# A segment-recurrent attention and ReGLU kernel laid out anew: leftover rows packed, transposes by DMA, memory sums in column quarters, an order searched offline

## The chip, the cores and the metric

The kernel runs on one core of a Trainium2 chip. The time is device microseconds of that core, taken over several executions. The profile is one execution recorded by the hardware profiler. PE is TensorE's matmul row, PEld its weight loads, DVE is VectorE, ACT ScalarE, POOL GpSimd, SP SyncE, whose queue issues the DMAs. A run on one core has no second die to compare with. All repeated runs here are recorded as of the fast state (granted clock 0.952 to 0.954 in the runs of the kernel before, 0.992 to 0.995 in those of the changed one); runs with a single execution are marked "one look", and their state is unknown.

Ratios are computed as the mean time of one kernel's runs over that of the other's of the same rounds, so they are not quite the ratio of the medians that are quoted.

## The reference, cut to what matters

```python
def _A_ref(x, mem0, Wq, Wk, Wv, Wo, seg_len):      # D = 448, H = 16 heads of 256, M = 8, seg_len = 32
    mem = mem0
    for s in range(n_seg):                          # 64 segments, one after the other
        h = concat([mem, x[:, s*32:(s+1)*32, :]])   # 40 rows
        q, k, v = h @ Wq, h @ Wk, h @ Wv
        p = softmax(where(mask, q @ k.T / 16, -1e9))
        o = (p @ v) @ Wo
        mem = o[:, :8, :]                           # the next segment needs it
        outs.append(o[:, 8:, :])
def _B_ref(x, W_gate, W_up, W_down):                # F = 1792
    gate = x @ W_gate
    return ((gate * (gate > 0)) * (x @ W_up)) @ W_down
x = x + _A_ref(layernorm(x), ...); x = x + _B_ref(layernorm(x), ...)    # layer 0
x = x + _A_ref(layernorm(x), ...); x = x + _B_ref(layernorm(x), ...)    # layer 1, the same weights
```

The eight memory rows make a recurrence over 64 segments. Everything else of a segment can wait. Both kernels form M = Wq Wk^T and N = Wv Wo per head during a setup phase. A step t then handles segment t of layer 0 together with segment t-4 of layer 1, so there are 68 steps. Two steps make a pair: 64 rows of each layer go through the sum over N and the gated unit together.

Names used below. `h` is a segment with its memory rows; `hT` is `h` with the features on the partitions, `hK` the same rows in natural layout, and T = M h. `Ps` and `Pm` are the softmax weights of the segment's rows and of the memory rows, `PTs` and `PTm` their transposes. U is these weights times `h`, before the sum over N (`Nw` in the trace); it lies in a large buffer called `big`, and the memory's own part in `UTm`. `XA` is the input of a layer's attention that is added back (the residual), `XB` is `XA` plus the attention's output, and `xn` and `xBT` are its LayerNorm, plain and transposed. The addition into XB ends a pair's sum over N and serves as the marker of a pair. A pitch is the time from one matmul's start to the next one's in an unbroken run. A change of tiling is a change of how the array is divided between matmuls. "Half clock" is time for which the trace's record of clock grants shows half the clock. A bias is a number added to the priority of one kind of group in the program's scheduler.

## The kernel before

The width 448 is three blocks of 128 rows and a leftover of 64. The kernel before pads the leftover with zeros to a fourth block (`kt = 3`):

```python
def t_unit(self, t, k):          # k = 0..6; T = M h for 8 of 56 blocks
    return [MM(v[:, j, l0 * KEYS:l0 * KEYS + n], S.M[:, kt, 8 * k + j, :],
               S.hT[:, pp, s, kt, l0:l1, :]..., start=(kt == 0), stop=(kt == 3))
            for j in range(8) for kt in range(4)]                      # 7 x 32 = 224 matmuls of 80 columns a step
```

The memory sum runs in four column tiles of the array; its four quarters are split into a high and a low half in bf16, and small matmuls with a selection matrix add and transpose them:

```python
def un_mem(self, t):
    for k in range(14):
        for j in range(4):
            o = 14 * j + k
            out.append(MM(b[32 * j:32 * j + 32, 0:D], lhs, S.N[:, o, :], start=(k == 0), stop=(k == 13)))
    ...
    S.act(... S.hi = copy of b ...)
    S.dve(... S.lo = b - S.hi ...)
def m_t(self, t): ...            # 8 matmuls selm x hi, lo: memory transposed, into the next hT
def m_nat(self, t): ...          # 2 matmuls of 448 columns with seln: memory in natural layout, into hK
```

The sum over N of a pair is 56 full matmuls, and all of them wait for all of U:

```python
def un(self, p):
    uk = [("U", s, l, c) for s in range(2) for l in range(2) for c in range(4)]
    for k in range(0, NO, 2):
        S.mm(lambda k=k: [MM(S.bO[:, 0:D], S.U[:, o, :], S.N[:, o, :], ...) for o in (k, k + 1)],
             2 * S.pitch(D), uk, S.ps(4))
```

Transposes of the LayerNorm outputs (`xn`), of the softmax weights (`Ps`) and, in the setup, of Wq, Wk and Wv are TensorE transposes with a copy out of PSUM each. PSUM is divided by hand: two pairs of banks for T, U and the gated unit (`R`), one bank for scores and transposes (`bG`), one for the long sums (`bO`), two for the memory (`bC`). A list scheduler in the program orders the groups once, when the kernel is built.

## Time and profile before

| | before |
|---|---|
| time, median | 1988.25 us (1987.97 to 1988.95, 3 runs) |
| PE / DVE / ACT busy | 92% / 51% / 39% of the span |
| first addition into XB (end of the setup and of pair 0) | 165.8 us |
| one pair of steps, mean of 24 steady pairs | 55.5 us |
| from the last XB to the end | 17.7 us |

The page's busy row and its strips, 40 equal slices of the span, the busy share in tenths (PEclk is the clock that the throttle granted):

```profile
PE 1825.2 (92%) x30992; PEld 1305.1 (66%) x30992; DVE 1013.9 (51%) x2529; ACT 771.0 (39%) x1960; POOL 94.3 (5%) x160
...
PE   7769999999999999999999999999999999999998
...
PEclk9869999999999999999999999999999999999999
```

TensorE is the bound, and only the setup is visibly thin. What a step costs TensorE is read from starts in the timeline: a matmul of 80 columns every 36.3 ns, of 448 every 190 ns. This is the timeline of TensorE at the turn from one pair to the next (start, duration, in brackets the idle time before it and who ended it):

```profile
1020.98 0.60 PE L127 MATMUL R<-PTs,hK 40*128 40x512 bf16 x4 [0.21 <-ACT PTs L709]
1022.96 0.39 PE L127 MATMUL R<-PTs,hK 40*128 40x512 bf16 x2 [1.38 <-DVE big L710]
1023.56 0.30 PE L127 MATMUL R<-PTs,hK 40*64 40x256 bf16 x4 [0.20 <-DVE big L710]
1024.71 1.65 PE L127 MATMUL bO<-Nw,big 128*128 128x448 bf16 x4 [0.85 <-DVE big L710]
```

Four waits within 4 us, 2.6 us in all; the last three are for copies of U (`big`). This returns in every pair; in the table of waits over the whole run it is the first two of these lines (total, times, longest; the third is a wait at another place, which section 1 needs):

```profile
PE R L127 <- DVE big L710: 47.4, 61, 1.4
PE bO L127 <- DVE big L710: 25.2, 31, 0.8
...
PE R L127 <- DVE xBT L710: 22.2, 32, 1.0
```

And this is the view of windows for the steady stretch from 500 to 1600 us (busy time of each engine, granted clock, DMA share, GB/s):

```profile
500.00:1600.00 1100.00, 1033.42 (x17910) 745.81 (x17908) 572.46 (x1404) 427.88 (x1094) 44.45 (x80) 0.96 0.02 4
```

TensorE is idle for 66.6 of 1100 us, 3.4 us a pair. The clock is 0.96 of full speed: the trace's record of clock grants has half-clock windows of 3.4 or 6.8 us about once a pair, 189 us of them in the whole run, 140 of these after the first 200 us (the setup has one of 27.3 us).

The windows lie on one grid of 3.41 us. From 300 us to 60 us before the end, 30 half-clock windows begin. In the 3.41 us of the grid just before, TensorE had stood idle for 1.65 to 2.44 us in 29 of these cases (0.94 in one); in no grid window that half clock did not follow had it been idle for more than 0.84 us. In this trace it is the sum of the short waits that sets the two kinds apart: no single wait between 300 and 1500 us was longer than 1.4 us.

### The profile page before, as it was taken

Reading aid. Unit: us, or ns where it says so; the run is one execution under the profiler, and the core shown is the slowest. Engines: PE = TensorE matmul, PEld = TensorE weight load, DVE = VectorE, ACT = ScalarE, POOL = GpSimd, SP = SyncE. Lnnn points to the kernel's source line nnn. Section 1 sums busy time; section 2 is a strip of 40 time slices with the busy share of each in tenths; the row PEclk is TensorE's granted clock in tenths of the full one; section 3 lists DMA queues with packets and bytes.
Section 4 is the critical chain, followed back from the end, with each engine's and each line's share of the span. In section 5 each row is a group of like instructions: output and inputs, shape, how many; then the busy total and the mean of one; then the engine's idle time right before and its main releaser. Section 6 shows DMA issues by size and latency. Waiting matters only on the chain.

```text
span 1986.3 us, 68251 instructions
## 1 busy us (share of the span) xinstructions
PE 1825.2 (92%) x30992; PEld 1305.1 (66%) x30992; DVE 1013.9 (51%) x2529; ACT 771.0 (39%) x1960; POOL 94.3 (5%) x160
## 2 busy tenths in 40 slices
PE   7769999999999999999999999999999999999998
PEld 5446776666666777666666677666666667766665
DVE  8623545554555544555554554455454555455432
ACT  6523333334343433333444443333344343333333
POOL 1020000000000000000000000000000000000000
PEclk9869999999999999999999999999999999999999
DMA  7400000000000000000000000000000000000000
GB/s 212 160 30 3 4 4 5 5 4 4 5 4 4 4 4 5 4 4 5 3 4 5 5 5 3 5 4 4 3 5 4 4 5 3 4 4 3 3 3 4
DMA packets 22303, 27.55 MB, mean 14 GB/s; under 512 B 5744, under 2 KB 15744, under 8 KB 22016
## 3 DMA queue, kind: packets, MB, share of 16 engines
q1 hardware_dynamic: 22016, 23.20, 4.0%
q8 instruction: 245, 4.01, 0.8%
q14 instruction: 42, 0.34, 0.1%
HBM read 21.35 MB, written 1.84 MB: 12 GB/s over the span
## 4 chain that ended last, share of the span: by engine, by line
PE 68%; DVE 17%; ACT 2%; issue 1%; DVEq 0%
PE R L127 35%; PE bO L127 22%; PE bC L127 8%; DVE big L710 7%; PE bG L127 2%; DVE stat L736 1%; DVE ys L1007 1%; DVE xn L743 1%; DVE XA L1003 1%; DVE hK L710 1%; DVE UTm L710 1%; DVE XB L978 1%; DVE Ps L870 1%; DVE hB L996 1%; DVE stat L868 1%
## 5 line engine op out<-in xcount | busy, mean ns | idle before, releaser
L127 PE MATMUL R<-hT,Mw 128*128 128x80 bf16 (+1 forms) x15232 | 548.7, 200 | 23.9 <-POOL hT L710 22.9
L127 PEld LDWEIGHTS R<-hT,Mw 128*128 128x128 bf16 x15232 | 539.7, 100 | 39.0 <-issue 24.0
L127 PE MATMUL bO<-Nw,big 128*128 128x448 bf16 x1904 | 463.5, 388 | 25.2 <-DVE big L710 25.2
L127 PEld LDWEIGHTS bO<-Nw,big 128*128 128x128 bf16 x1904 | 180.5, 105 | 201.4 <-issue 66.4
L127 PE MATMUL R<-xBT,big 128*128 128x128 bf16 x3808 | 251.7, 220 | 22.9 <-DVE xBT L710 22.2
L996 DVE TENSOR_TENSOR hB<-gT,R 128x256 bf16<-128x256 bf16 x238 | 100.0, 420 | 325.4 <-ACT gT L995 322.4
L127 PEld LDWEIGHTS R<-xBT,big 128*128 128x128 bf16 x3808 | 224.6, 98 | 46.2 <-DVE xBT L710 27.7
L127 PE MATMUL bC<-Nw,UTm 128*32 128x448 bf16 x3752 | 194.8, 360 | 3.0 <-ACT UTm L709 1.9
L709 ACT ACTIVATE TTs<-R 128x512 bf16<-128x512 f32 (+3 forms) x273 | 155.1, 568 | 107.8 <-PE R L127 107.8
L710 DVE CAST TTs<-R 128x512 bf16<-128x512 f32 (+3 forms) x271 | 176.4, 651 | 8.7 <-PE R L127 8.5
L995 ACT ACTIVATE gT<-R 128x256 bf16<-128x256 f32 x238 | 91.2, 383 | 183.4 <-PE R L127 179.5
L709 ACT ACTIVATE big<-R 128x512 bf16<-128x512 f32 (+1 forms) x263 | 134.6, 543 | 63.3 <-PE R L127 61.9
L710 POOL COPY hK<-xn 32x448 bf16<-32x448 bf16 x136 | 75.5, 555 | 1710.6 <-DVE xn L743 1659.1
L710 DVE CAST big<-R 128x512 bf16<-128x512 f32 (+1 forms) x249 | 148.7, 619 | 14.6 <-PE R L127 12.5
L710 DVE CAST TTm<-R 128x128 bf16<-128x128 f32 (+3 forms) x278 | 78.0, 281 | 151.2 <-PE R L127 138.8
L127 PEld LDWEIGHTS bC<-Nw,UTm 128*32 128x32 bf16 x3752 | 99.8, 98 | 83.6 <-ACT UTm L709 13.8
L127 PE MATMUL R<-PTs,hK 40*128 40x512 bf16 (+1 forms) x640 | 95.4, 352 | 57.8 <-DVE big L710 47.4
L709 ACT ACTIVATE hK<-bC 8x448 bf16<-8x448 f32 x96 | 51.4, 535 | 202.1 <-PE bC L127 200.5
L127 PE MATMUL bO<-big,hB 128*128 128x448 bf16 x476 | 129.2, 354 | 0.0
L127 PEld LDWEIGHTS R<-PTs,hK 40*128 40x128 bf16 (+1 forms) x640 | 26.4, 98 | 136.4 <-ACT big L709 57.7
L920 DVE TENSOR_TENSOR lo<-bC,hi 128x448 bf16<-128x448 f32 x67 | 41.5, 620 | 131.2 <-ACT hi L919 131.2
L709 ACT ACTIVATE TTm<-R 128x128 bf16<-128x128 f32 (+3 forms) x266 | 70.5, 265 | 70.6 <-PE R L127 70.6
(125 smaller groups left out, 1540.9 us busy)
## 6 DMA issues: line engine op xcount, KB each, us to landing
big<-in_A_Wo_dram SPq DMA_DIRECT2D x4, 896.0 KB, 5.7
big<-in_A_Wq_dram SPq DMA_DIRECT2D x4, 768.0 KB, 6.0
big<-in_A_Wk_dram SPq DMA_DIRECT2D x4, 768.0 KB, 7.8
big<-in_A_Wv_dram SPq DMA_DIRECT2D x4, 768.0 KB, 5.1
XA<-in_A_x_dram SPq DMA_DIRECT2D x32, 56.0 KB, 2.2
out_dram<-ys SPq DMA_DIRECT2D x32, 56.0 KB, 1.9
big<-in_B_W_down_dram SPq DMA_DIRECT2D x1, 1568.0 KB, 14.7
big<-in_B_W_gate_dram SPq DMA_DIRECT2D x1, 1344.0 KB, 7.3
```

The source lines that it names most:

```text
L127: ins = E.matmul(out, lhsT=lhsT, rhs=rhs, **kw)
L709: return E.activation(out(), src(), ACT.Copy)
L710: return E.tensor_copy(out(), src())
L736: S.dve(lambda E: E.bn_stats(st[:, so:so + 6], x), D, rd, [(key, 0)])
L743: S.dve(lambda E, a=a, b=b, src=src: E.tensor_scalar(S.xn[:, i, a:b], src, st[:, so + 6:so + 7], st[:, so + 8:so + 9], op0=ALU.subtract, o ...
L868: S.dve(lambda E: E.tensor_reduce(st[:, 48:48 + n], Sm, AX.X, ALU.add), w, [("Sm",)], [("ss", 1)])
L870: S.dve(lambda E: E.tensor_tensor(dst, Sm, bc(56), ALU.mult), w, [("Sm",), ("ss", 2)], [("Ps",)])
L920: S.dve(lambda E: E.tensor_tensor(S.lo[:, :], b[:, 0:D], S.hi[:, :], ALU.subtract), D, S.ps(6) + [("hi",)], [("lo",)])
L978: S.dve(lambda E: E.tensor_tensor(S.XB[:, p % 2, :], S.bO[:, 0:D], S.XA[:, p % 4, :], ALU.add), D, S.ps(4) + [("XA", p % 4, 0), ("XA", p % ...
L995: S.act(lambda E, k=k, R=R: E.activation(S.gT[:, k % 2, 0:256], R.b(0)[:, 0:256], ACT.Relu), 256, R.res(0), [("gT", k % 2)])
L996: S.dve(lambda E, k=k, R=R: E.tensor_tensor(S.hB[:, 2 * k:2 * k + 2, :].rearrange("p a b -> p (a b)"), S.gT[:, k % 2, 0:256], R.b(1)[:, 0: ...
L1003: S.dve(lambda E: E.tensor_tensor(S.XA[64:128, q % 4, :], S.bO[0:64, 0:D], S.XB[0:64, p % 2, :], ALU.add), D, S.ps(4, half=(0,)) + [("XB", ...
```

## The change

The same redesign is carried through in one step: leftover rows are packed in pairs, transposes move to DMA, the memory sums use column quarters, in 14 odd pairs the layer-1 sums ride along in spare columns, all eight PSUM banks form one pool, and the order is steered by biases per kind of group that were searched offline. The core of the diff, with cuts:

```diff
 # T units: 28 blocks x 2 heads; the leftover 64 rows of two heads side by side in the two halves of the array
-                    for j in range(8) for kt in range(4)]
+            def hm(Ts=Ts, a=a, z=z, o=o):
+                return [MM(o(Ts[st], j - a), S.M3[64 * st:64 * st + 64, j, :], hv(slice(64 * st, 64 * st + 64), 3 + st), start=(j == a))
+                        for j in range(a, z) for st in range(2)]
+                    return [MM(o(T, j - a), S.M[:, c, st, j, :], hv(full, c), stop=(c == 2)) for j in range(a, z) for c in range(3)]
...
 # memory sums
-            for k in range(14):
-                for j in range(4):
-                    o = 14 * j + k
-                    out.append(MM(b[32 * j:32 * j + 32, 0:D], lhs, S.N[:, o, :], start=(k == 0), stop=(k == 13)))
-        S.act(lambda E: E.activation(S.hi[:, :], b[:, 0:D], ACT.Copy), D, S.ps(6), [("hi",)])
-        S.dve(lambda E: E.tensor_tensor(S.lo[:, :], b[:, 0:D], S.hi[:, :], ALU.subtract), D, S.ps(6) + [("hi",)], [("lo",)])
+            return [MM(T.b()[32 * j:32 * j + 32, 0:224], S.UTm[:, o, :], S.N[:, o, 224 * (j % 2):224 * (j % 2) + 224], start=(k == 0), stop=(k == 27))
+                    for k in range(28) for j in range(4) for o in (28 * (j // 2) + k,)]
+        S.act("xE", lambda E: E.activation(S.XH[64:128, :], T.b()[64:128, 0:224], ACT.Copy), 224, T.res(BOTQ), [("XH",)])
+        for j in range(2):
+            S.dve("xE", ... S.X[r, c] = T.b()[r, 0:224] + S.XH[r2, :] ...)
...
 # transposes by DMA: hT to hK, Ps to PTs, xn to stg and xBT; in the setup Wq, Wk, Wv
+        S.dma("pts", "pts", lambda E: E.dma_start_transpose(S.PTs[:, :, :], S.Ps[:, :, :].rearrange("p a b -> p (a b)")), [("Ps",)], [("PTs",)],
+              1310.0, 2550.0)
...
 # sums over N: wait per chunk of U; in odd pairs only layer 0, two terms side by side, layer 1 rides in UTm[:, :, 16:32]
-        uk = [("U", s, l, c) for s in range(2) for l in range(2) for c in range(4)]
+                     2 * S.pitch(D), [("U", l, s, c_of(k)) for l in range(2) for s in range(2)] + nk, T.res())
+                S.mm("unc", lambda k=k: [MM(T.b()[64 * w:64 * w + 64, 0:D], S.U[:, o + w, cols], S.N[:, o + w, :], ...)
+                                         for o in (k, k + 2) for w in range(2)], ..., mode=COLS2)
...
 # the order, and waits that another wait implies are left out
+        for o in self.ops:
+            o.prio += BIAS.get(o.kind, 0.0)
+BIAS = {"dn": -2542.0, "dnE": -32472.0, ..., "lnaT": 13146.0, ..., "ys": 19174.0}
+            out.append((self.sems[src].sem, val))
+            for s2, v2 in self.clock[(src, val)].items():
+                if kn.get(s2, 0) < v2:
+                    kn[s2] = v2
```

The gated unit packs its leftover rows in the same way (98 instead of 112 matmul pitches).

## The prediction

> **What bounds the kernel now.** TensorE. In the page's busy row PE has 92% of the span, DVE 51%, ACT 39%. The XB additions (timeline) put the first at 165.8 us; then a pair of steps takes 55.3 us almost without variation, and 17.7 us follow the last. From matmul starts in the timeline (80 columns 36.3 ns, 128: 56, 448: 190, 40: 25), one step's own matmuls need 14.0 us: T units 224 x 36.3 = 8.1, memory sums 2.8, segment scores 0.9, U products 0.9, hi/lo copies and transposes the rest. A pair adds 10.6 (sums over Nw), 6.3 (gate/up), 2.7 (down), 0.5 (transposes): 48 us. About 18 changes of tiling at some 0.1 us (gap 1128.57 to 1128.68) make 50. The other 5.5 us are idle waits (XB, bank evictions before bO) and the halved clock (mean 0.94 to 0.96 in the windows).
>
> **What the change does, per steady pair.**
> - T units: the 64 leftover rows of D are row-packed, 224 full matmuls become 168 and 28 packed pairs: 7.1 instead of 8.1 us, -2.1 a pair. The trace shows such packing working: two row tiles (PTs,hK) start 3 ns apart. [...]
> - Gate/up the same way: 112 become 98 pitches, -0.8.
> - All transposes but Pm's, and the hi/lo gather, leave TensorE for DMA transposes and an fp32 addition: about -1.9.
> - Odd pairs: layer 1's rows ride in 16 unused columns of the memory sums, and layer 0's are column-packed: 28 pitches instead of 56, -2.6 on average.
> - Memory sums: 28 rounds of four 224-column tiles instead of 14 of 448: 2.7, unchanged. 112 small weight loads fit if they issue 3 ns apart as now.
> - More changes of tiling: 26 a pair in the built order, +0.7.
> Work falls from 50 to 43.5 us a pair, all on the PE path.
>
> **Other engines.** Evictions and softmax sum to about 25 us a step over DVE and ACT, some 12 of 23.5 each: not a bound. The recurrence, from hT to the next hT, is about 17 us with today's durations: shorter than a step. DMA transposes have no duration in this trace; [...] loads of x land in 2.2 us here. At 2 to 3 us they hide behind the T units.
>
> **Setup.** Now PE spends 384 transposes there with their evictions and ends in a 22.9 us wait (111 us)[...]. DMA transposes of Wq, Wk, Wv remove this; with Wo they move about 15 MB. First XB at 97 us, an estimate, instead of 166.
>
> **Sum.** 97 + 37 (second pair, one layer) + 30 x 46.6 + 72 (last two) + 17: about 1620 us, with 3 us a pair left for waits and clock instead of 5.5, since eight single banks and a searched order should leave fewer bank waits. If the 5.5 stay, 1695; with almost none, 1540.
>
> **What would show it.** Matmul group of hT,Mw down to 168 a step at the same 36 ns pitch; M3 pairs starting 3 ns apart; pairs alternating about 44 and 49 us; first XB near 97 us; transposes landing under 3 us; PE busy over 90% in the steady part and the chain of waits mostly PE.
>
> **What would make it wrong.** DMA transposes of 5 us or more, which lengthen the recurrence (hK before u, xBT before gate); column tiles of 224 limited by weight loads[...]; more half-clock windows from short PE gaps; a setup limited by slow DMA transposes of weights. None costs the 350 us saved.
>
> Chances: faster 0.97, same 0.02, slower 0.01.

## The result, and the profile after

The changed kernel takes 1567.84 us (1567.33 to 1569.21, 4 runs) against 1988.51 us in the same rounds: ratio 0.789, 95% interval 0.788 to 0.790. It is correct. The page of after, the lines that answer to those of before:

```profile
PE 1486.0 (95%) x33352; PEld 1150.6 (73%) x33352; DVE 710.6 (45%) x1892; ACT 808.3 (52%) x2388; POOL 91.0 (6%) x139
...
PE   3989999999999999999999999999999999999997
...
PEclk9899999999999999999999999999999999999999
```

The view of windows, 300 to 1400 us:

```profile
300.00:1400.00 1100.00, 1069.33 (x24233) 838.52 (x24233) 505.63 (x1328) 577.69 (x1687) 68.69 (x99) 1.00 0.18 27
```

TensorE is now idle for 30.7 of 1100 us, which is 1.25 us of a pair's 44.7 us, and the clock is full. Half-clock windows add up to 25.6 us in the run, where they were 189; none lies between 300 and 1500 us, where TensorE is idle for at most 1.7 us of any 3.41 us of the grid. No sharp limit can be read from the two traces: 1.65 to 2.44 us of idle time came before 29 of 30 half-clock windows there, and up to 1.7 us is followed by none here. The packed leftover rows in the timeline:

```profile
848.92 0.82 PE L134 MATMUL P<-hT,M 64*128 64x80 bf16 x36 [0.79 <-POOL hT L568]
849.67 4.04 PE L134 MATMUL P<-hT,Mw 128*128 128x80 bf16 x108
```

The 36 packed matmuls start in couples 3 to 4 ns apart, one couple every 36 ns, so 18 couples take 0.65 us; then 0.1 us passes to the next tiling (its first start is at 849.67).

The setup shows one fault. This is the timeline of the DMA queue (start, issue time):

```profile
1.39 3.53 SPq L624 DMA_TRANSPOSE big<-in_A_Wq_dram  x1
15.41 1.20 SPq L728 DMA_TRANSPOSE stg<-xnA  x1
16.65 3.55 SPq L624 DMA_TRANSPOSE big<-in_A_Wk_dram  x1
20.24 3.96 SPq L624 DMA_TRANSPOSE big<-in_A_Wq_dram  x1
```

Here the queue does not pass a waiting entry. Its third entry is the transpose of the first LayerNorm's output, which is not ready until 15.4 us, and the transposes of the weights stand behind it from 4.9 to 15.4 us. The first product starts at 22.3 us.

Where the 421 us went, by the XB additions in the timeline:

| stretch | before, us | after, us | estimate in the prediction, us |
|---|---|---|---|
| start to the first XB | 165.8 | 123.1 | 97 |
| first to second XB | 53.3 | 31.5 | 37 |
| second to last XB | 1749.4 | 1397.8 | 30 x 46.6 and 72 for the last two pairs, 1470 |
| last XB to the end | 17.7 | 14.9 | 17 |

### The profile page after: what moved, and what is told of

Same layout as the page of the kernel before. It is cut to its first block, busy times and chain, and to the rows that moved or that the text cites. A ratio compares the mean times of both kernels' runs of the same rounds, so it can differ in the third digit from the quotient of the medians.

```text
span 1567.3 us, 72227 instructions
## 1 busy us (share of the span) xinstructions
PE 1486.0 (95%) x33352; PEld 1150.6 (73%) x33352; DVE 710.6 (45%) x1892; ACT 808.3 (52%) x2388; POOL 91.0 (6%) x139
## 4 chain that ended last, share of the span: by engine, by line
PE 78%; DMA 10%; DVE 6%; ACT 3%; issue 1%; SPq 1%; POOL 1%; POOLq 0%; DVEq 0%
PE P L134 78%; DMA stg<-xnA 4%; DMA PTs<-Ps 4%; ACT big L567 2%; DVE big L568 1%; SPq L624 1%; DVE stat L714 1%; DMA xBT<-xnB 1%; POOL hT L568 1%; DVE xnA L721 1%; DVE XA L1070 0%; DVE ys L1073 0%; DMA big<-in_A_Wk_dram 0%; DMA big<-in_B_W_down_dram 0%; ACT Mw L567 0%
## 5 line engine op out<-in xcount | busy, mean ns | idle before, releaser
L134 PE MATMUL P<-hT,Mw 128*128 128x80 bf16 (+1 forms) x11424 | 425.5, 200 | 4.1 <-issue 4.0
L134 PEld LDWEIGHTS P<-hT,Mw 128*128 128x128 bf16 x11424 | 405.1, 100 | 13.5 <-issue 4.6
L134 PE MATMUL P<-Nw,big 128*64 128x448 bf16 (+1 forms) x1904 | 305.2, 355 | 0.7 <-DVE big L568 0.5
L567 ACT ACTIVATE TTs<-P 128x384 bf16<-128x384 f32 (+3 forms) x612 | 275.4, 450 | 3.0 <-PE P L134 2.9
L567 ACT ACTIVATE TTm<-P 128x96 bf16<-128x96 f32 (+2 forms) x613 | 148.6, 242 | 153.8 <-PE P L134 148.6
L567 ACT ACTIVATE big<-P 128x512 bf16<-128x512 f32 (+1 forms) x351 | 173.6, 546 | 71.7 <-PE P L134 70.1
L134 PE MATMUL P<-xBT,big 128*128 128x128 bf16 (+3 forms) x3808 | 199.0, 216 | 3.4 <-DMA xBT<-xnB 3.3
L134 PEld LDWEIGHTS P<-Nw,big 128*64 128x64 bf16 (+1 forms) x1904 | 127.2, 104 | 102.1 <-issue 11.5
L134 PEld LDWEIGHTS P<-xBT,big 128*128 128x128 bf16 (+1 forms) x3808 | 181.1, 98 | 19.4 <-issue 5.8
L134 PE MATMUL P<-Nw,UTm 128*32 128x224 bf16 x7504 | 193.7, 261 | 1.2 <-ACT UTm L567 1.2
L134 PEld LDWEIGHTS P<-Nw,UTm 128*32 128x32 bf16 x7504 | 176.1, 97 | 24.2 <-ACT UTm L567 12.5
L134 PEld LDWEIGHTS P<-hT,M 64*128 64x128 bf16 x3808 | 73.9, 96 | 45.1 <-POOL hT L568 21.6
```

Source lines behind the costliest of these rows:

```text
L134: ins = E.matmul(out, lhsT=lhsT, rhs=rhs, **kw)
L567: return E.activation(out(), src(), ACT.Copy)
```

## The experiments

Twelve kernels were run. All gave correct results. Pair times are means over some 24 steady pairs, from XB additions; "half clock" is the sum of the trace's half-clock windows.

### 1. The kernel before with one line of the change: waits per chunk of U

```diff
-        uk = [("U", s, l, c) for s in range(2) for l in range(2) for c in range(4)]
         for k in range(0, NO, 2):
+            uk = [("U", s, l, k // 16) for s in range(2) for l in range(2)]
```

> The kernel before, with one part of the change: each pair of matmuls of the sum over Nw waits for the U columns that it reads, not for all of U of both steps. In the profile of before, TensorE stood idle about 2.6 us at the start of these sums in every pair and half-clock windows of 3.4 to 6.8 us followed once a pair (189 us in all). Theory (that gap is what drops the clock): gap and half-clock windows both go, 2 to 4.5 us a pair, 1835 to 1920 us, half-clock time under 80 us. Rival (the windows have another cause, or the wait turns up elsewhere): above 1930 us, half-clock time above 130 us.

Measured: 1868.06 us (1867.81 to 1869.69, 4 runs), ratio to before 0.940 (0.939 to 0.941). A pair takes 51.7 us instead of 55.5. The windows of 500 to 1600 us:

```profile
500.00:1600.00 1100.00, 1068.49 (x19142) 791.50 (x19141) 611.00 (x1485) 463.06 (x1190) 48.93 (x88) 1.00 0.02 5
```

and the waits of this run that answer to those of before:

```profile
PE bO L127 <- ACT big L709: 20.3, 32, 0.7
...
PE R L127 <- DVE xBT L710: 1.6, 3, 0.5
```

Idle fell from 3.4 to 1.5 us a pair, the clock rose from 0.96 to 1.00, and half clock fell from 189 to 51 us; of the 51, 7 come after the first 200 us, where there had been 140. The order shifted too, since it is computed from the same dependencies: the waits for xBT, 0.6 us a pair, went as well. No matmul was added or removed. So 120 us came from one over-wide wait and the order that it had forced: 1.9 us a pair of idle, and about as much again of halved clock that followed it. The theory holds; the rival needed more than 130 us of half clock to remain. The changed kernel has the finer wait too. What the coarse wait would cost there was not run, so its share of that kernel's gain is inferred.

### 2. Packing undone, first try: the loop order turned

```diff
-                        for j in range(a, z) for st in range(2)]
+                        for st in range(2) for j in range(a, z)]
```

> The changed kernel with one loop order turned in the T units: all matmuls of the upper 64 rows first, then all of the lower 64 rows, so that two row tiles never run side by side. Same matmuls, same order of groups, same waits. Theory (the packing pays because two row tiles run at once and TensorE is the bound): 28 more pitches of 36 ns in each of 60 two-layer steps and 28 of 25 ns in 8 one-layer steps, so about +66 us, near 1634 us, with hT,M starts about 36 ns apart instead of in pairs. Rival (weight loads or issue bound it, packing is idle capacity): under +15 us.

Measured (one look): 1584.04 us, +16. That looks like the rival, but the experiment had not done what it was meant to do. These are the first starts of one unit in the trace (us; a is the upper half of the array, b the lower, assigned by the 36 ns spacing; program order is six a, six b, six a, six b):

```
a 813.978  a 814.017  a 814.058  b 814.066  a 814.093  b 814.104  a 814.129  b 814.145  a 814.165 ...
... a 814.201  b 814.217  a 814.237  b 814.253 (carries the semaphore increment, 12th in the program)
```

By this assignment the two halves each kept their own order and ran side by side anyway. The twelfth matmul of the program, which the trace marks by its semaphore increment, is the fourteenth to start. In 58 of the 60 runs of three whole units in this trace the increments stand on the 14th, 26th and 36th start; in the changed kernel, with the loop order a, b, a, b, such runs have them on the 12th, 24th and 36th. Only the first and last few of each run stand alone. So this run says nothing of the value of packing, and a second was made.

### 3. Packing undone: full 128-row matmuls

The other half of the weights meets zeros that lie in hT already, so the result is the same. The order of all groups is unchanged.

```diff
-S.M3[64 * st:64 * st + 64, j, :], hv(slice(64 * st, 64 * st + 64), 3 + st)
+S.M3[:, j, :], hv(full, 3 + st)
```

> The first run did not undo the packing: the two row tiles still interleaved in the trace. Here the T units' 64 leftover rows use full 128-row matmuls (the other half of the same weights meets zeros that already lie in hT), in the same order and with the same waits, so nothing runs side by side and no change of tiling is needed around them. Theory: 28 more pitches a step, 1.0 us, +66 us over the run, less about 0.2 us for each of the 2 to 3 packed groups of a step whose change of tiling goes away (some 30 us): +25 to +45 us, 1595 to 1615 us. Rival (packing costs as much in changes of tiling as it saves): 1560 to 1575 us.

Measured: 1607.40 us (1606.14 to 1608.57, 4 runs), +39.6; ratio to before 0.809 (0.808 to 0.810), where the changed kernel has 0.789. The matmuls now start singly every 36 ns. Packing pays, and the net is what the count gives: 66 us of matmul pitches less some 27 us, which fits the 221 changes of tiling that the trace of this run has fewer (656 instead of 877), at about 0.1 us each. A pair takes 45.9 us instead of 44.7.

### 4. Riding undone, with the biases as they were, and with none

Odd pairs sum both layers with 56 full matmuls, as even pairs do; nothing rides.

```diff
     def rider(t):
-        return (p, g) if 3 <= p <= 29 else None
+        return None
     def rides(p):
-        return p % 2 == 1 and 3 <= p <= 29
+        return False
 # and the outputs go where the kernel's own even pairs put theirs
```

> The changed kernel without riding rows: odd pairs sum both layers over Nw with 56 full matmuls as even pairs do, and the spare columns of the memory sums stay zero. Theory: 14 pairs get 28 pitches of 190 ns more, 5.3 us each, +74 us, near 1640 us, less a few us for tiling changes saved and the RN/RT work gone. Rival (the riders' waits and copies give part of it back): +30 us or less. The biases were searched for the riding order, so an excess over +74 would be that.

Measured (one look): 1710.33 us, +142, with 118 us of half clock and pairs of 49.5 us.

The second kernel removes the biases too:

> No riding rows and no order biases. The biases were searched for the riding order, so without riding they may harm; here both sides of the comparison (this against the run without biases, 1638.75 us) have the plain order. Theory (riding saves TensorE work of 5.3 us in 14 pairs, the rest of the +142 us was the misfit of the biases and the half clock it brought): +55 to +95 us over 1638.75, 1695 to 1735 us. Rival (riding is worth about 140 us whatever the order, by shortening waits too): 1760 us or more.

Measured (one look): 1807.47 us, +169 over the riding kernel without biases (section 6), with 220 us of half clock. The first run missed both sides, upward; in the second the rival's figure was met. Riding seemed worth twice the TensorE work it saves. But in both the extra was visible as waits, 58 us for xBT and 48 us for Pm in the second one, and as half clock. An order fitted to the graph might hide them. That is a question that only a searched order can answer.

### 5. Riding undone, order searched anew

4046 trials with the kernel's own order model, starting from the changed kernel's values.

```diff
-BIAS = {"dn": -2542.0, "dnE": -32472.0, ...}
+BIAS = {...}    # searched for this graph; also RESERVE, SLACK, MODEPEN
```

> No riding rows, with biases, slack, reserve and mode penalty searched anew for this graph with the kernel's own order model (4046 trials, from the changed kernel's values). The first two runs without riding gave +142 us (biases of the riding order) and +169 us over the other run without biases, against 74 us of TensorE work counted. Theory (the excess was waits and half clock from an unsuited order): now +55 to +85 us over the changed kernel, 1623 to 1653 us, half-clock time under 60 us. Rival (riding takes a dependency away that no order hides): 1670 us or more.

Measured: 1601.39 us (1600.38 to 1601.67, 4 runs), +34; ratio 0.805 (0.804 to 0.807). Both sides missed: it is less than the theory's lower end. Two things explain it. First, this order no longer lets the first LayerNorm block the DMA queue, so its first XB comes at 113.5 instead of 123.1 us; counted from there, riding is worth about 44 us. Second, the windows of the steady part:

```profile
300.00:1400.00 1100.00, 1087.65 (x23582) 842.28 (x23580) 487.28 (x1313) 540.15 (x1534) 21.77 (x48) 1.00 0.15 25
```

A pair takes 46.0 us, of which TensorE idles 0.5; in the changed kernel 44.7, of which it idles 1.25. So riding saves about 2.0 us of TensorE's time a pair (2.65 by the count of pitches, less 3.6 changes of tiling, 26.2 against 22.6 a pair in the traces, that the order without riding does not need) and gives back about 0.7 as waiting. The excess of section 4 was the unsuited order. One thing stays open: the changed kernel's own order was not searched again with as many trials, so a part of the 34 to 44 us can be the search and not riding.

### 6. The order without biases

```diff
-BIAS = {"dn": -2542.0, ...}
+BIAS = {}
```

> The changed kernel with all order biases per kind removed (slack, reserve and mode penalty kept): the plain critical-path order over the same graph and the same banks. Theory A (the searched order is what closes TensorE's gaps and with them keeps the clock up): at least 3 us a pair come back, +100 us or more, and half-clock windows come back (25.6 us in the changed kernel, 189 us before). Theory B (single banks and less work suffice): under +50 us, half-clock time under 60 us.

Measured (one look): 1638.75 us, +71, half clock 84 us. It lies between the two theories. A pair takes 46.6 to 47.8 us, by the 24 pairs chosen, instead of 44.7, so the searched order is worth 2 to 3 us a pair in the steady part. But this kernel is 19.6 us ahead at the first XB (103.6 against 123.1 us), though that marker moves with the order; by the third XB it is 15 us ahead (186.2 against 201.2). About 10 us of the lead are the head of the DMA queue: without biases the first product starts at 10.3 us, in the changed kernel at 22.3 (section 7). That the searched biases bought the steady part at the expense of the rest of the setup would be the next guess; section 11 tried it, on section 9's order, and saw no gain.

### 7. The head of the DMA queue in the setup

```diff
-        S.dma("lnaT", "lnA", lambda E: ...
+        S.dma("lnaT" if p else "lnaT0", "lnA", lambda E: ...
-BIAS = {..., "lnaT": 13146.0, ...}
+BIAS = {..., "lnaT": 13146.0, "lnaT0": -1000.0, ...}
```

> The changed kernel with the bias of the first LayerNorm's DMA transpose alone lowered, so that it stands behind the eight transposes of Wq and Wk on the in-order SP queue instead of second. In the changed kernel the queue stood from 4.9 to 15.4 us for it. Theory (setup is bound by that queue, and the wait at its head delays everything): first product 10 us earlier (about 12 instead of 22.3 us), first XB near 113 instead of 123.1 us, time 1558 us, about 10 us or 0.6% less. Rival (evictions of the products, or Wv and Wo, bound the setup): under 3 us.

Measured: 1560.68 us (1559.73 to 1562.28, 5 runs), ratio to before 0.785 (0.784 to 0.786); the interval does not overlap that of the changed kernel. The timeline of the DMA queue:

```profile
1.39 3.50 SPq L624 DMA_TRANSPOSE big<-in_A_Wq_dram  x1
4.94 3.83 SPq L624 DMA_TRANSPOSE big<-in_A_Wk_dram  x1
8.80 4.00 SPq L624 DMA_TRANSPOSE big<-in_A_Wq_dram  x1
```

The first product starts at 11.0 us, the first XB comes at 113.2 us, 10 us earlier as expected, and the last XB 9.6 us earlier. Of that, 7.2 us show in the median. The tail of the profiled run is 1 us longer; the rest of the difference was not traced.

### 8. Memory sums as four quarters of the terms instead of column quarters

```diff
-MM(T.b()[32 * j:32 * j + 32, 0:224], S.UTm[:, o, :], S.N[:, o, 224 * (j % 2):224 * (j % 2) + 224], start=(k == 0), stop=(k == 27))
-    for k in range(28) for j in range(4) for o in (28 * (j // 2) + k,)
+MM(T.b()[32 * j:32 * j + 32, 0:D], S.UTm[:, o, :], S.N[:, o, :], start=(k == 0), stop=(k == 13))
+    for k in range(14) for j in range(4) for o in (14 * j + k,)
 # cut: the copy and the two additions that follow become 448 wide, too
```

> The memory sums as four quarters of the terms with all 448 columns in each column tile (14 rounds, as in the kernel before) instead of two halves of the terms by two halves of the columns (28 rounds of 224). Same order of all groups. TensorE work the same within 0.03 us a step; the copy of two quarters and the two additions that close the memory chain become 448 wide instead of 224, about 0.2 us longer each, 0.4 to 0.7 us a step on the recurrence. Theory (the recurrence has slack behind other TensorE work): under +12 us. Rival (the recurrence is on the chain in every step): +27 to +47 us over 68 steps.

Measured: 1586.50 us (1580.08 to 1589.65, 4 runs, the widest spread of all), +18.7; ratio 0.798 (0.796 to 0.799). It lies between the two. The addition grew from 382 to 616 ns, and it is made twice a step. In the table of waits a line became large that was small in the changed kernel (the first line here is the changed kernel's, the second this run's):

```profile
PE P L134 <- DVE X L910: 2.9, 4, 1.3
PE P L134 <- DVE X L910: 25.7, 56, 1.9
```

By the durations the memory chain grew by about 0.7 us a step, 1.4 a pair. In the steady part some 30% of that reached the time: a pair takes 45.1 instead of 44.7 us, 11.5 us over 28 pairs. The first XB comes 6 us later, and that is another thing: from 80 to 130 us this trace has 13.6 us of half clock where the changed kernel's has 3.4, which is worth about 5 us. So the recurrence is neither hidden nor bounding: most of a longer chain is absorbed, and not all of it. Column quarters were worth 1.2% here, some 0.7% by the shorter chain and not by TensorE's work, which is the same.

### 9. Ps transposed on TensorE again, order searched anew

```diff
-        S.dma("pts", "pts", lambda E: E.dma_start_transpose(S.PTs[:, :, :], ...), [("Ps",)], [("PTs",)], 1310.0, 2550.0)
+        T2 = S.tile()
+        S.mm("ptm", lambda: [TR(T2.b().bitcast(BF)[:, a * 128:a * 128 + 128], S.Ps[:, a, :], S.ident[:, :]) for a in range(4)],
+             4 * S.pitch(128), [("Ps",), ("ident",)], T2.res())
+        S.cp("pts", lambda: S.PTs..., lambda: T2.b().bitcast(BF)[:, 0:512], 512, T2.res(), [("PTs",)])
```

> The segment weights' transposes (Ps to PTs, 68 of them) go back from the DMA queue to TensorE, as in the kernel before: four 128x128 transposes and one copy of 512 columns a step; biases searched anew for this graph. TensorE gets 0.22 us a step more, 15 us in all, DVE or ACT 0.6 us a step more; the waits for this DMA (14.6 us of TensorE's idle time in the changed kernel) go. Theory A (TensorE's work decides): +10 to +25 us, 1578 to 1593 us. Theory B (the DMA's latency costs as much as it saves): within 8 us of 1568. The two are close, since A less the waits is near B.

Measured: 1559.54 us (1556.88 to 1561.15, 4 runs), -8; ratio 0.784 (0.783 to 0.785). At first sight theory A is wrong by its sign. But this order, too, lets the weights go first in the queue: its third XB comes at 195.4 us, 5.8 us earlier than in the changed kernel, and after it the pairs take 44.6 against 44.7 us. So the move itself is worth about 2 us: theory B, a tie. TensorE's busy time rose from 1069.3 to 1076.4 of 1100 us; the waits for this DMA, the first line here (changed kernel), are gone. The second line is the windows of this run:

```profile
PE P L134 <- DMA PTs<-Ps: 14.6, 15, 1.6
300.00:1400.00 1100.00, 1076.42 (x24508) 851.34 (x24507) 533.28 (x1407) 580.60 (x1652) 70.28 (x100) 1.00 0.13 21
```

### 10. Waits that others imply, put back

Same order on every engine, checked instruction by instruction.

```diff
             out.append((self.sems[src].sem, val))
-            for s2, v2 in self.clock[(src, val)].items():
-                if kn.get(s2, 0) < v2:
-                    kn[s2] = v2
```

> The changed kernel with the same order on every engine, checked instruction by instruction, but without leaving out waits that another wait already implies: 1883 semaphore waits on TensorE instead of 1690, 1701 instead of 1474 on ScalarE, 1984 instead of 1622 on VectorE. In the changed kernel's trace a separate wait instruction took about 50 ns on TensorE's queue, mostly ahead of time. Theory (they run ahead in the queue and cost nothing): within 5 us. Rival (each delays a matmul group by its 50 ns): 193 more on TensorE, up to +10 us, more with the other engines.

Measured: 1569.04 us (1566.75 to 1569.95, 4 runs), +1.2, within the spread. The separate wait instructions on TensorE rose from 445 to 548 in the trace and cost nothing that can be measured. This part of the change is neutral.

### 11. A better version? Setup without biases

```diff
-            o.prio += BIAS.get(o.kind, 0.0)
+            o.prio += (EARLY if o.i < self.early else BIAS).get(o.kind, 0.0)    # EARLY = {}: setup and first step
+        free["dve"] = 13300.0                                                    # the order model's start
```

> The kernel with Ps transposed on TensorE and its searched biases (1559.5 us), but with no biases for the setup and the first step, and with the order model told that VectorE is busy with constants for 13.3 us. The idea comes from the run without biases: there the third pair's first XB came at 186.2 us, here at 195.4, in the changed kernel at 201.1 us. Theory (biases searched for the steady part misplace the setup): 3 to 9 us less, 1550 to 1557 us. Rival (setup is bound by the DMA of the weights, whose queue already never stands): within 2 us of 1559.5.

Measured: 1561.16 us (1558.16 to 1563.02, 5 runs), ratio 0.785 (0.784 to 0.786), no better than section 9's 1559.54. The rival holds. Sections 7 and 9 are the fastest found, about 1560 us, 0.5% below the changed kernel, and they do not differ from each other within their spread.

## Why the prediction was right or wrong, point by point

The time was forecast at 1620 us (1550 to 1705) with 0.97 for faster; it is 1567.84. The range held it, near its fast end, and two errors of opposite sign stand behind that: a setup 26 us longer than estimated made up for part of a steady stretch 72 us shorter. So the distance of 52 us owes something to luck.

- **"Work falls from 50 to 43.5 us a pair, all on the PE path": right.** In the steady windows TensorE is busy 1069.3 of 1100 us, 43.4 us of a pair's 44.7. Undoing parts one at a time gives the terms: packing of T +39.6 us (section 3; 1.2 us a pair, the predicted 2.1 less its changes of tiling), riding +34, or 44 with the setup evened out (section 5). The packing of gate/up, the end of the hi/lo gather, and the DMA transposes of xn and of the weights were not undone one by one, so their terms are counted and not shown. The term "-2.6 on average" for riding was right for TensorE's pitches, but about 0.6 of it goes to changes of tiling and 0.7 is given back as waiting; the prediction booked the changes of tiling in a line of their own and no waiting to riding.
- **"With 3 us a pair left for waits and clock instead of 5.5": the mis-sized term.** It measured 1.25 us, all idle, at full clock. The prediction had taken the halved clock as a cost that only shrinks, along with the bank waits. Section 1 shows that it hung on one gap a pair, made by an over-wide wait: with the gap gone the half-clock time fell from 189 to 51 us, without any other part of the change. The finer wait alone does not keep the clock up, though: without its biases the changed kernel has 84 us of half clock again (section 6). A pair came out at 44.7 instead of 46.6 us; over 30 pairs that is some 58 us of the 72 by which the second to the last XB came out shorter than the estimate.
- **"First XB at 97 us, an estimate": wrong, 123.1 us.** Ten of the 26 us are the DMA queue standing behind the first LayerNorm (section 7). The prediction gives no working for its 97, and no wait of the queue. It named "a setup limited by slow DMA transposes of weights" as a danger; of the rest it can be said that the queue in section 7, which never stands, is still issuing weights until 64 us, and the first memory sum starts at 75.8. That is a reading of the timeline, not an experiment.
- **"The recurrence ... about 17 us ... shorter than a step": not measured, and too comfortable.** Section 8 lengthened it by about 0.7 us a step, and in the steady part some 30% of that came through. A chain shorter than the step by that estimate still cost 0.4 us a pair when it was lengthened (45.1 instead of 44.7).
- **"Eight single banks and a searched order should leave fewer bank waits": right for the order**, 2 to 3 us a pair (section 6). The single banks were not tested alone.
- **"Transposes landing under 3 us": mostly.** Ps takes 2.4, xBT 2.4, xn 3.0, hK 3.3 us in the median. The prediction's 2 to 3 us was the author's estimate; in the trace of before the plain loads of x land in 2.2 us. Of the large ones, 896 KB of Wo, a plain load, land in 5.6 us, transposed quarters of Wq and Wk of the same size in 5.9 and 6.1, but those of Wv, issued between loads of Wo, in 8.8. And a transpose of this size holds the issuing queue for 3.5 to 4.0 us (Wq, Wk) and for up to 6.5 us (Wv), where the plain load of Wo holds it for 0.58; the transposes of Ps, xBT and hT hold it for 1.2 us in the median, that of xn for 1.3.
- **"Memory sums ... 2.7, unchanged", "112 small weight loads fit": right.** In the timeline 112 matmuls of 224 columns take 2.87 us from the first start to the end of the last, where 56 of twice the width take 2.83 in section 8's kernel.
- **"Pairs alternating about 44 and 49 us": not seen**, and it could not be, since the searched order moves the long sums across the pair's boundary. XB additions come 13 to 51 us apart in a pattern of two or four pairs. A mean over many pairs was the right marker.

## What to carry to other kernels

When the bounding engine shows 9s in nearly every slice, still look for a small idle spot that returns at the same place in each round, and add up short waits that lie close together, because here 1.9 us of waiting a pair cost as much again in halved clock; the cure was one dependency made as fine as the data. Count what a packing or a riding trick saves net of its changes of tiling and of the order it needs, and compare designs only after each has had its own order searched: the same removal measured +142, +169 and +34 us. An order tuned offline against a model still has to be read in the trace, from its first entry on: here ten microseconds stood at the head of a DMA queue.
